# Second mixture in two halves of the tokens with 512 columns a matmul, and keys and receptances on GpSimd at the start

## The chip, the core and the metric

The kernel runs on one core of one Trainium2 chip. The metric is the device time of one execution in microseconds (us). The engines are TensorE (PE, its weight loads PEld), VectorE (DVE), ScalarE (ACT), GpSimd (POOL) and SyncE (SP), whose queue issues the DMAs.

## The reference

Three stages follow one another. `B, H, S, D = 4, 8, 768, 48`, so there are 3072 tokens of 384 features.

```python
for t in range(S):
    cur = einsum('bhd,bhe->bhde', u * kt, vt)
    y[:, :, t] = einsum('bhd,bhde->bhe', rt, state + cur)
    state = wt[..., None] * state + einsum('bhd,bhe->bhde', kt, vt)
x = y.transpose(0, 2, 1, 3).reshape(3072, 384)
x = ((x @ w1) * (x @ w2)) @ w3 @ w_out
P = exp(x @ w_gate - max)
for _ in range(8):
    P /= P.sum(1) + 1e-9; P /= P.sum(0) + 1e-9; P *= 3072 / 8
out = sum(P[:, e:e+1] * (relu(x @ ew1[e]) @ ew2[e]) for e in range(8))
```

The first mixture has 1024 hidden units; each of the 8 experts of the second has 1024 as well.

## The kernel before

**The start.** The recurrence is worked in 24 chunks of 128 tokens, and the first mixture in 8 blocks of 384 tokens. Their steps are issued in 107 slices. For the first 28 slices the table `START` (line 26) writes the order out by hand, a token a step: `L` loads an input, `ld`, `lw`, `ex`, `jn` bring a 64-bit weight to float32 (DMA, ScalarE, ScalarE, VectorE), `w34` multiplies w3 by w_out on TensorE, `scanF`, `scanG`, `small`, `ks`, `rp`, `kx`, `rx` make the decayed keys and receptances of a chunk, `sc`, `trn`, `yt1`, `up`, `yt2` are its matmuls. `ks` (line 291) and `rp` (line 296) run on VectorE, and `kx` and `rx` (from line 301) on GpSimd read what they made. The order in the program is each engine's own order: an engine that waits holds all that stands behind it.

**The second mixture.** x @ ew1 is computed as a product of two 3x3 block matrices by 15 products (`ORDER`, with the factors in `WA` and `XC`) and not 27. Each factor is split into a high and a low part in fp32r, and each product is three matmuls (high by high, high by low, low by high). The factors of x, high and low, are made once by `pre_x`, written to DRAM (`xd`) and loaded back in four groups of up to four products (`ld_x` into `xc`). The factors of w1 are made by `sp_w1` for one pair of blocks of hidden units at a time: sums on GpSimd, high parts on ScalarE, low parts on GpSimd.

A **phase** `n` works on 768 tokens (`sb`, one of 4 sets) and on two blocks of hidden units of 3 x 128 (`k`). There are 64 phases. `x2[sb]` holds a set as 9 tiles of T = 256 tokens: 3 blocks of features by 3 blocks of tokens. Each of the 15 products of a phase is two times three matmuls of 256 columns, one triple for either block of hidden units, side by side in one bank of PSUM (`z_prod`, tile `zp`; four banks). ScalarE (`cp`) and VectorE (`add`, `sub`) fold the products into the hidden layer, `h_hi` (ScalarE) and `h_lo` (VectorE) take its positive part and split it. Between the products of phase n stand the units of phase n-1 (`y_fill`): a unit is three matmuls of 384 columns, and four units close one accumulator `yp` of 128 tokens, which VectorE adds to `acc` (line 1064). There are 24 units a phase and three banks for `yp`. `later` and `spread` hang other work on the count of products done: making the weights, loading factors (`release` after each group of four products), and the gate's iteration (`sk`) in the first phases.

Of the kernel before, what the change touches and what calls it, by code (L numbers as in the profile page):

```python
# [30 lines left out]
w34.0.4 L.rn.2 kn.0 L.k.3 cp.0 w34.0.5 ex.5.0 jn.4.1 yt1.0 up.0 ex.5.1 scanF.2 w34.0.6 lw.5 w34.0.7 Sn.0 jn.5.0
yt2.0 lw.6 ld.8 L.r.3 L.rn.3 small.2 w34.1.0 L.w.3 cc.1 xraw.0 L.kn.3 sc.1 rp.2 L.v.2 jn.5.1 ex.6.0 rx.2 trn.1
w34.1.1 ws.0 ec.1 w34.1.2 jn.6.0 lw.7 w34.1.3 rk.2 cp.1 w34.1.4 ex.6.1 kn.1 w34.2.0 jn.6.1 ex.7.0 w34.1.5 w34l.0
w34.2.1 jn.7.0 lw.8 ld.10 w34.1.6 L.kn.4 ld.9 yt1.1 scanG.2 ex.8.0 w34.2.2 ex.7.1 w34.1.7 ks.2 w34.2.3 ws.1 jn.7.1
kx.2 w34.2.4 w34.2.5 w34l.1 jn.8.0 w34.3.0 ld.11 L.rn.4 w34.2.6 scanF.3 w34.2.7 ex.8.1 w34.3.1 ws.2 jn.8.1 w34.3.2
up.1 cc.2 ld.12 w34.4.0 lw.9 L.r.4 Sn.1 rk.3 w34.3.3 L.v.3 L.w.4 ex.9.0 w34.3.4 lw.10 jn.9.0 w34.3.5 ec.2 sc.2
ex.9.1 yt2.1 cc.3 scanG.3 w34.4.1 w34.4.2 lw.12 small.3 w34.4.3 rp.3 w34.3.6 xraw.1 cp.2 rx.3 w34.4.4 jn.9.1 ex.12.0
trn.2 w34l.2 lw.11 w34.4.5 jn.12.0 w34.3.7 ld.13 L.k.4 ex.10.0 w34.4.6 ks.3 ws.3 w34.4.7 jn.10.0 kx.3 L.k.5 ex.12.1
w34.5.0 L.kn.5 ws.4 L.w.5 w34.5.1 w34l.3 jn.12.1 ex.10.1 w34.5.2 rk.4 kn.2 jn.10.1 w34.5.3 ex.11.0 yt1.2 w34.5.4
jn.11.0 ex.11.1 ld.14 ec.3 L.r.5 up.2 hi.0 L.kn.6 w34.6.0 L.rn.6 Sn.2 ex.13.0 lo.0 w34.5.5 lw.13 w34.6.1 jn.11.1  # L40
w34.5.6 w34l.4 yt2.2 w34.6.2 jn.13.0 xraw.2 ld.16 w34.5.7 ld.15 scanF.4 ex.13.1 sc.3 xd.2 ws.5 w34.6.3 jn.13.1 trn.3
lw.14 w34l.5 w34.6.4 scanG.4 ex.14.0 w34.6.5 hi.1 w34.7.0 jn.14.0 L.w.6 kn.3 w34.6.6 lo.1 xh.0 w34.7.1 cp.3 w34.6.7
lw.16 small.4 w34.7.2 xl.0 yt1.3 ex.14.1 w34.7.3 ws.6 ks.4 up.3 ex.15.0 jn.14.1 kx.4 L.k.6 w34.7.4 L.v.4 w34.7.5
rp.4 hi.2 ld.17 L.v.5 w34.7.6 Sn.3 L.rn.5 lw.15 lo.2 L.r.6 w34.7.7 ex.16.0 pa.0.0 ws.7 jn.15.0 w34l.6 yt2.3 ex.15.1
jn.16.0 rx.4 asb.0.0 jn.15.1 pb.0.0 w34l.7 scanF.5 hi.3 pa.0.1 ex.16.1 lo.3 lw.17 cc.4 gs.0.0 sc.4 xraw.3 jn.16.1
# [14 lines left out]
def tile_rwkv_moe_sinkhorn_moe(  # L60
# [592 lines left out]
    def sp_w2(i):  # L653
# [3 lines left out]
        k = i % 4  # L657
        pool = pools["m" if k < 2 else "m2"]
        hi = pool.tile([P, 2, DM], F32R, tag=f"w2h{k}", name=f"w2h{k}")
        lo = pool.tile([P, 2, DM], F32R, tag=f"w2l{k}", name=f"w2l{k}")  # L660
# [34 lines left out]
    def pre_group(sb, g, tag, tmp_, eng):  # L695
        t = pools["w"].tile([P, 2, len(XP_[g][4]), T], F32R, tag=tag, name="xpre")
        sums, high, low = factors(XP_, g, XB, x2[sb], tmp_, t, eng)

        def end():
            low()  # L700
            xd[sb, g] = dram.tile(list(t.shape), F32, name=f"xd{sb}{g}")
# [535 lines left out]
```

## Time and profile before

| what | us |
|---|---|
| runs, median (lowest to highest of 3) | 1956.44 (1955.25 to 1956.48) |
| the profiled execution, its own time | 1958.0 |
| its span | 1956.2 |
| TensorE matmul busy | 1926.2 |
| VectorE, ScalarE, GpSimd busy | 1380.6, 685.7, 632.1 |
| start of the first phase of the second mixture | 446.2 |

Span is the time from the first to the last instruction; the profiled execution's own time is 1.8 us longer. TensorE's matmuls overlap, so the spacing of their starts tells what one costs, not its own duration. The granted clock is that of TensorE, as a share of 2.4 GHz.

### The profile page before, as it was taken

What the parts mean: (1) busy time and instruction counts of PE and PEld (TensorE: products, weight loads), DVE (VectorE), ACT (ScalarE), POOL (GpSimd) and SP (SyncE); (2) the same over time, 40 slices, a digit from 0 to 9 for tenths busy, and PEclk for the clock granted to TensorE, in tenths of its full rate; (3) what the DMA queues carried; (4) which work ended last, traced back from release to release, by engine and by line L of the source; (5) the groups of instructions that cost most, each with busy time, mean ns of one, the idle gap of its engine ahead of it and who ended that gap; (6) DMA issues with size and microseconds to landing.
All of it is one profiled execution on the core that took longest, in us unless ns stands there. A gap on an engine that the chain in (4) does not pass through costs nothing.

```text
span 1956.2 us, 38114 instructions
## 1 busy us (share of the span) xinstructions
PE 1926.2 (98%) x15499; PEld 1865.7 (95%) x15499; DVE 1380.6 (71%) x2419; ACT 685.7 (35%) x1320; POOL 632.1 (32%) x859
## 2 busy tenths in 40 slices
PE   6999999999999999999999999999999999999999
PEld 3689999999999999999999999999999999999999
DVE  8865777765787786666767676666676767667665
ACT  5733333344333333333323333333333333333322
POOL 4666666635331313122222222221313231312200
PEclk9999999999999999999999999999999999999999
DMA  9623444346645555555555555545455555555453
GB/s 366 219 85 96 140 132 137 103 148 240 230 171 187 186 192 192 178 198 182 194 188 187 178 199 182 190 173 204 170 195 183 190 187 190 190 178 183 171 199 120
DMA packets 90494, 353.76 MB, mean 181 GB/s; under 512 B 10384, under 2 KB 34256, under 8 KB 64592
## 3 DMA queue, kind: packets, MB, share of 16 engines
q1 hardware_dynamic: 90320, 351.34, 51.7%
q8 instruction: 122, 2.00, 0.4%
q14 instruction: 52, 0.43, 0.1%
HBM read 329.67 MB, written 20.45 MB: 179 GB/s over the span
## 4 chain that ended last, share of the span: by engine, by line
PE 94%; DMA 2%; DVE 2%; ACT 1%; issue 0%; SPq 0%; POOL 0%; DVEq 0%; ACTq 0%
PE yp L112 40%; PE zp L112 34%; PE pa L112 5%; PE po L112 5%; PE pb L112 5%; PE yt L112 1%; DMA raw<-in_moe_w_dram 1%; PE trn L112 1%; PE sc L112 1%; PE up L112 1%; DMA raw<-in_moe_w_out_dram 0%; PE w34ps L112 0%; DVE ct L892 0%; DMA nat_r<-in_rt_dram 0%; PE pl L112 0%
## 5 line engine op out<-in xcount | busy, mean ns | idle before, releaser
L112 PE MATMUL zp<-xc,w1c 128*128 128x256 f32 x5760 | 839.5, 282 | 2.0 <-DVE ct L895 1.1
L112 PEld LDWEIGHTS zp<-xc,w1c 128*128 128x128 f32 x5760 | 790.7, 188 | 16.9 <-DVE ct L895 2.9
L112 PE MATMUL yp<-w2h,hl 128*128 128x384 f32 x1536 | 516.6, 336 | 0.5 <-DVE hl L889 0.5
L112 PE MATMUL yp<-w2h,hh 128*128 128x384 f32 x1536 | 517.1, 337 | 0.0
L112 PE MATMUL yp<-w2l,hh 128*128 128x384 f32 x1536 | 514.1, 335 | 0.0
L884 ACT ACTIVATE hh<-ct 128x512 fp32r<-128x512 f32 x384 | 236.9, 632 | 601.9 <-DVE ct L895 329.0
L892 DVE TENSOR_TENSOR ct<-ct,zp 128x512 f32<-128x512 f32 x576 | 380.9, 684 | 58.1 <-PE zp L112 57.5
L614 POOL TENSOR_TENSOR w1c<-w1s,w1c 128x512 fp32r<-128x512 f32 (+1 forms) x120 | 127.2, 1060 | 787.6 <-PE zp L112 475.7
L899 ACT ACTIVATE ct<-zp 128x512 f32<-128x512 f32 x256 | 153.4, 599 | 397.9 <-PE zp L112 393.9
L112 PEld LDWEIGHTS yp<-w2h,hh 128*128 128x128 f32 x1536 | 290.7, 189 | 0.2 <-issue 0.2
L112 PEld LDWEIGHTS yp<-w2h,hl 128*128 128x128 f32 x1536 | 288.1, 188 | 0.9 <-DVE hl L889 0.8
L112 PEld LDWEIGHTS yp<-w2l,hh 128*128 128x128 f32 x1536 | 288.5, 188 | 0.0
L889 DVE SCALAR_TENSOR_TENSOR hl<-ct,hh 128x512 fp32r<-128x512 f32 x384 | 273.8, 727 | 0.0
L1064 DVE SCALAR_TENSOR_TENSOR acc<-yp,Pm,acc 128x384 f32<-128x384 f32 x336 | 205.3, 611 | 69.9 <-PE yp L112 69.8
L895 DVE TENSOR_TENSOR ct<-ct,zp 128x512 f32<-128x512 f32 x128 | 88.1, 688 | 170.2 <-PE zp L112 170.1
L895 DVE TENSOR_TENSOR ct<-zp,ct 128x512 f32<-128x512 f32 x128 | 88.4, 691 | 135.9 <-PE zp L112 131.0
L614 POOL TENSOR_TENSOR w1c<-w1raw,w1c 128x128 fp32r<-128x128 f32 (+1 forms) x90 | 55.0, 611 | 221.4 <-ACT w1c L610 221.4
L606 POOL TENSOR_TENSOR w1s<-w1raw 128x128 f32<-128x128 f32 x240 | 120.1, 521 | 0.2
L481 POOL TENSOR_TENSOR gl<-gs,gh 128x384 fp32r<-128x384 f32 x64 | 73.3, 1147 | 111.1 <-ACT gh L477 111.1
L112 PE MATMUL pa<-xhl,w1h 128*128 128x384 f32 x384 | 102.2, 347 | 0.0
L112 PE MATMUL pb<-xhl,w2h 128*128 128x384 f32 x384 | 98.9, 338 | 2.3 <-DVE cv L228 2.3
L472 DVE TENSOR_TENSOR gs<-pb,asb 128x384 f32<-128x384 f32 x64 | 35.4, 554 | 72.3 <-PE pb L112 52.7
(128 smaller groups left out, 1900.6 us busy)
## 6 DMA issues: line engine op xcount, KB each, us to landing
xc<-xd SPq DMA_DIRECT2D x192, 1024.0 KB, 4.9
xc<-xd SPq DMA_DIRECT2D x64, 768.0 KB, 4.3
xd<-x2s SPq DMA_DIRECT2D x53, 256.0 KB, 2.9
w1raw<-in_e_w_dram SPq DMA_DIRECT2D x32, 384.0 KB, 3.1
w2raw<-in_e_w_dram SPq DMA_DIRECT2D x32, 384.0 KB, 3.1
raw<-in_moe_w_dram SPq DMA_DIRECT2D x8, 1024.0 KB, 8.5
nat_w<-in_w_dram SPq DMA_DIRECT2D x24, 264.5 KB, 3.5
nat_k<-in_kt_dram SPq DMA_DIRECT2D x24, 256.0 KB, 4.1
```

The costliest lines, as they stand in the source:

```text
L112: nc.tensor.matmul(o, lhsT, rhs, start=start, stop=stop, **kw)
L472: nc.vector.tensor_tensor(t, m_t.pop(("pb", blk, f)), m_t.pop(("asb", blk, f)), op=ALU.mult)
L481: nc.gpsimd.tensor_tensor(gl[:, f, :], m_t.pop(("gs", blk, f)), gh[:, f, :].bitcast(F32), op=ALU.subtract)
L606: eng.tensor_tensor(tmp_[:, many.index(r), :], at_(a), at_(b), op=ALU.add if sg == 1 else ALU.subtract)
L614: eng.tensor_tensor(lo[:, d0:d1, :], sv, hi[:, d0:d1, :].bitcast(F32), op=ALU.subtract)
L884: nc.scalar.activation(hh, src, AF.Relu)
L889: nc.vector.scalar_tensor_tensor(hl, src, 0.0, hh.bitcast(F32), op0=ALU.max, op1=ALU.subtract)
L892: nc.vector.tensor_tensor(o, a, b_, op=ALU.add)
L895: nc.vector.tensor_tensor(o, a, b_, op=ALU.subtract)
L899: nc.scalar.activation(t, src, AF.Copy)
L1064: nc.vector.scalar_tensor_tensor(dst, yp, so["Pm"][:, tt, e:e + 1], dst, op0=ALU.mult, op1=ALU.add)
```

## The change

The second mixture now works on two sets of 1536 tokens (`SS = 2 * S`) with T = 512, and a phase has one block of hidden units `p`. `SEQ` lists the 64 phases: two blocks on one set, the same two on the other, then the next two blocks starting from the set at hand, so the factors of x are loaded at every second phase and shared by two. A product is three matmuls of 512 columns. A unit of `y_fill` is still three matmuls of 384 columns, and two of them close an accumulator, of which there are 12 a phase. The even ones go to VectorE as before. The odd ones (but for the last phase's) go through ScalarE, scaled by the gate, into one of two pieces of a work tile `xw`, and GpSimd adds that to `acc`. The weights' factors have two sets, not three, and w1's and w2's raw tiles one, not two; one set's factors of x are made on VectorE during the first mixture, the other's on VectorE and, from slice 90 into the third phase, on GpSimd.

At the start `ks` and `rp` of the first five chunks go to GpSimd, the two copies of the unit block go to ScalarE, and `START` is another list.

```diff
+KS_POOL = (0, 1, 2, 3, 4)
+RP_POOL = (0, 1, 2, 3, 4)
 START = """
-L.w.0 L.w.1 L.k.0 ld.0 L.r.0 ld.1 L.kn.1 L.k.1 L.r.1 scanG.0 scanF.0 ks.0 scanG.1 lw.0 ld.2 ld.3 L.kn.0 ex.0.0
...
+L.w.0 L.k.0 ld.0 L.w.1 L.r.0 ld.1 scanG.0 scanF.0 ks.0 ex.0.0 ld.2 small.0 ld.3 lw.0 L.kn.0 scanG.1 L.rn.0 rp.0
...
-    T = 256
-    NR = S // T
-    NS = B
+    T = 512
+    SS = 2 * S
+    NR = SS // T
+    NS = NT // SS
...
-        nc.gpsimd.tensor_copy(eye[64 * c:64 * c + 64, :], ident[64 * c:64 * c + 64, 64 * c:64 * c + 64])
+        nc.scalar.activation(eye[64 * c:64 * c + 64, :], ident[64 * c:64 * c + 64, 64 * c:64 * c + 64], AF.Copy)
...
-        nc.vector.tensor_tensor(diag(t), nat["k", n % 2].rearrange("p (a b s) -> p b a s", b=2, s=32), gv, op=ALU.mult)
+        (nc.gpsimd if n in KS_POOL else nc.vector).tensor_tensor(diag(t), nat["k", n % 2].rearrange("p (a b s) -> p b a s", b=2, s=32), gv, op=ALU.mult)
...
+    SEQ = [(2 * k + j, sb) for k in range(NB2) for sb in ((0, 1), (1, 0))[k % 2] for j in range(2)]
+    N = len(SEQ)
...
+    B_DVE = (2, 13, 7, 9)
...
+    B_AT = {6: (90.75, 91.75, 92.75, 2), 15: (93.75, 94.75, 95.75, 3), 8: (99.25, 99.5, 100.75, 2),
+            5: (101.25, 101.5, 102.75, 3), 2: (100.75, 102.25, 103.25, 0), 13: (102.75, 104.25, 105.25, 1),
+            7: (104.75, 106.25, 107, 0), 9: (114, 115, 116, 0), 10: (114, 114, 115, 1), 11: (123, 124, 125, 1),
+            1: (119, 123, 124, 0), 12: (127, 130, 131, 1), 4: (126, 129, 130, 0), 3: (133, 136, 137, 1),
+            14: (132, 135, 136, 0)}
...
-        return pools["z"].tile([P, 2, T], F32, tag="z", bufs=4, name="zp")
+        return pools["z"].tile([P, T], F32, tag="z", bufs=4, name="zp")
...
-        xt = xc[n, g]
-        for j in range(2):
-            wt = w1c[(n // NS) * 2 + j, g]
-            for c, (a_, b_) in enumerate(((0, 0), (0, 1), (1, 0))):
-                mm(bank[:, j, :], wt[:, a_, wi, :], xt[:, b_, xi, :], start and j == 0 and c == 0,
-                   stop and c == 2, skip=True)
+        wt, xt = w1c[SEQ[n][0], g], xc[n, g]
+        for c, (a_, b_) in enumerate(((0, 0), (0, 1), (1, 0))):
+            mm(bank, wt[:, a_, wi, :], xt[:, b_, xi, :], start and c == 0, stop and c == 2, skip=True)
...
+                two = t % 2 and n < N - 1
...
+                elif two:
+                    yt_n[0] += 1
+                    c0 = T * (yt_n[0] % 2)
+                    tm = xw_part(c0, c0 + DM)
+                    if e == 0:
+                        nc.scalar.activation(tm, yp, AF.Copy)
+                    else:
+                        nc.scalar.activation(tm, yp, AF.Copy, scale=so["Pm"][:, tt, e:e + 1])
+                    nc.gpsimd.tensor_tensor(dst, dst, tm, op=ALU.add)
...
     def release(n, g):
...
-        ld_x(n + 1, g)
-        if sb == NS - 1:
-            spread(1, 3 if g == 2 else 2, sp_w1(2 * k + 3, g, nc.gpsimd))
+        p, sb = SEQ[n]
+        if n + 1 < N:
+            if SEQ[n + 1][1] == sb:
+                xc[n + 1, g] = xc[n, g]
+            elif n == 1 and g > 1:
+                later(29 + g - at["slot"], lambda: ld_x(n + 1, g))
+            else:
+                ld_x(n + 1, g)
+        if n % 4 > 1 and p + 2 < NW:
+            spread(12 if p % 2 else 1, 3, lazy(lambda: sp_w1(p + 2, g, nc.gpsimd)))
```

TensorE's order inside a late phase, with the z matmuls (`zp`) of two products and the units of the phase before it between them. Before:

```order
L112 MATMUL zp<-xc_19674,w1c_19084 128x256 x3
L112 MATMUL zp<-xc_19674,w1c_19677 128x256 x3
L112 MATMUL yp<-w2h_18174,hh 128x384
L112 MATMUL yp<-w2l_18175,hh 128x384
L112 MATMUL yp<-w2h_18174,hl 128x384
L112 MATMUL zp<-xc_19674,w1c_19084 128x256 x3
```

With the change:

```order
L115 MATMUL zp<-xc_16211,w1c_16440 128x512 x3
L115 MATMUL yp<-w2h,hh 128x384
L115 MATMUL yp<-w2l,hh 128x384
L115 MATMUL yp<-w2h,hl 128x384
L115 MATMUL zp<-xc_16211,w1c_16440 128x512 x3
```

Two triples of 256 columns, with the weights of two blocks, became one triple of 512 columns with one block's weights; the units between them are the same.

ScalarE's order in a late phase, where `hh` is the hidden layer's high half, `ct` a product taken out of PSUM, `w1c` weights and `xw` the work tile. Before:

```order
L899 ACTIVATE ct<-zp 128x512 x4
L610 ACTIVATE w1c_21538<-w1s 128x512
L884 ACTIVATE hh<-ct 128x512 x2
```

With the change:

```order
L912 ACTIVATE ct<-zp 128x512
L620 ACTIVATE w1c_18174<-xw 128x512
L1083 ACTIVATE xw<-yp,Pm 128x384
L897 ACTIVATE hh<-ct 128x512 x2
L1083 ACTIVATE xw<-yp,Pm 128x384
L897 ACTIVATE hh<-ct 128x512
L620 ACTIVATE w1c_18224<-w1raw 128x128
L620 ACTIVATE w1c_18224<-w1s 128x384
```

The copies of the odd accumulators (`xw<-yp,Pm`) now stand between the products, weights and hidden halves.

GpSimd's order at the very start, where `Kt` and `Rt` are a chunk's keys and receptances. Before:

```order
L136 AFFINE_SELECT mask<-mask 64x64
L304 TENSOR_TENSOR Kt<-Kt,Mt 128x8x32
L304 TENSOR_TENSOR Kt<-Kt,Ft 128x8x32
L310 TENSOR_TENSOR Rt<-Rt,Mt 128x8x32
L310 TENSOR_TENSOR Rt<-Rt,Ft 128x8x32
```

With the change:

```order
L139 AFFINE_SELECT mask<-mask 64x64 x2
L297 TENSOR_TENSOR Kt<-nat_k_101,Gt 128x2x8x32
L301 TENSOR_TENSOR Rt<-nat_r_99,Ft 128x2x8x32
L307 TENSOR_TENSOR Kt<-Kt,Mt 128x8x32
L307 TENSOR_TENSOR Kt<-Kt,Ft 128x8x32
L313 TENSOR_TENSOR Rt<-Rt,Mt 128x8x32
L313 TENSOR_TENSOR Rt<-Rt,Ft 128x8x32
```

The first chunk's `ks` (`Kt<-nat_k`) and `rp` (`Rt<-nat_r`) now stand on GpSimd ahead of the four halves that read them; on VectorE they are gone.

## Rows read from the trace of the kernel before

**Rows 1.** The page: engines, busy us (share) and instructions; shares of the ending chain.

```profile
PE 1926.2 (98%) x15499; PEld 1865.7 (95%) x15499; DVE 1380.6 (71%) x2419; ACT 685.7 (35%) x1320; POOL 632.1 (32%) x859
...
PE 94%; DMA 2%; DVE 2%; ACT 1%; issue 0%; SPq 0%; POOL 0%; DVEq 0%; ACTq 0%
```

**Rows 2.** Stretches: us, each engine's busy us (instructions), granted clock, DMA share, GB/s.

```profile
core 0: us, PE busy (x) PEld busy (x) DVE busy (x) ACT busy (x) POOL busy (x), PEclk, DMA share, GB/s
...
80.00:90.00 10.00, 7.68 (x91) 7.14 (x91) 9.13 (x19) 7.64 (x16) 9.21 (x9) 0.83 0.57 179
...
110.00:120.00 10.00, 8.81 (x222) 7.67 (x220) 6.49 (x20) 4.07 (x9) 9.92 (x12) 1.00 0.30 86
120.00:446.20 326.20, 326.20 (x3873) 308.31 (x3873) 227.58 (x485) 122.12 (x286) 183.78 (x174) 1.00 0.38 121
446.20:600.00 153.80, 151.53 (x1053) 147.80 (x1052) 114.99 (x219) 57.19 (x116) 62.29 (x92) 1.00 0.63 220
600.00:1900.00 1300.00, 1299.84 (x9078) 1287.93 (x9076) 903.59 (x1460) 420.91 (x775) 311.01 (x509) 1.00 0.53 187
1000.00:1200.00 200.00, 200.00 (x1397) 198.35 (x1396) 140.40 (x224) 66.22 (x124) 52.52 (x87) 1.00 0.54 188
```

**Rows 3.** TensorE in order of time, a late phase: start us, us, what.

```profile
1501.57 0.34 PE L112 MATMUL yp<-w2h,hh 128*128 128x384 f32 x1
...
1502.62 0.87 PE L112 MATMUL zp<-xc,w1c 128*128 128x256 f32 x6
1503.32 0.34 PE L112 MATMUL yp<-w2h,hh 128*128 128x384 f32 x1
```

**Rows 4.** TensorE in order of time, the end, 39 steps from first to last.

```profile
1945.57 0.33 PE L112 MATMUL yp<-w2h,hl 128*128 128x384 f32 x1
...
1952.33 0.34 PE L112 MATMUL yp<-w2h,hl 128*128 128x384 f32 x1
```

**Rows 5.** Groups, whole span: what, count | busy us, mean ns | idle before, releasers.

```profile
L1064 DVE SCALAR_TENSOR_TENSOR acc<-yp,Pm,acc 128x384 f32<-128x384 f32 x336 | 205.3, 611 | 69.9 <-PE yp L112 69.8
L606 POOL TENSOR_TENSOR w1s<-w1raw 128x128 f32<-128x128 f32 x240 | 120.1, 521 | 0.2
L481 POOL TENSOR_TENSOR gl<-gs,gh 128x384 fp32r<-128x384 f32 x64 | 73.3, 1147 | 111.1 <-ACT gh L477 111.1
L614 POOL TENSOR_TENSOR w1c<-w1s,w1c 128x512 fp32r<-128x512 f32 x30 | 39.4, 1314 | 787.6 <-PE zp L112 475.7 <-ACT w1c L610 311.9
L468 ACT ACTIVATE asb<-pa 128x384 f32<-128x384 f32 x64 | 31.4, 491 | 42.6 <-PE pa L112 39.5 <-DVE gs L472 3.1
L319 POOL TENSOR_TENSOR ec<-eye,cc 128x512 f32<-128x512 f32 x24 | 29.7, 1236 | 7.6 <-PE po L112 7.6
L294 DVE TENSOR_TENSOR Kt<-nat_k,Gt 128x512 f32<-128x512 f32 x24 | 18.1, 756 | 0.1
L298 DVE TENSOR_TENSOR Rt<-nat_r,Ft 128x512 f32<-128x512 f32 x24 | 17.1, 712 | 0.6 <-DMA nat_r<-in_rt_dram 0.6
```

**Rows 6.** TensorE in order of time, the first 84 us, where it stood still.

```profile
10.83 1.13 PE L112 MATMUL sc<-Rt,Kt 64*64 64x64 f32 x32 [10.83 <-POOL Rt L310]
...
19.41 6.97 PE L112 MATMUL w34ps<-wo,w3c 128*128 128x384 f32 x12 [6.40 <-DVE w3c L228]
...
30.97 0.91 PE L112 MATMUL w34ps<-wo,w3c 128*128 128x384 f32 x2 [1.39 <-DVE w3c L228]
...
83.10 0.96 PE L112 MATMUL pb<-xhl,w2h 128*128 128x384 f32 x2 [2.32 <-DVE cv L228]
```

**Rows 7.** ScalarE in order of time, its first instruction.

```profile
8.44 1.28 ACT L209 ACT_TABLE_LOAD   x1 [8.44 <-DMA raw<-in_moe_w_out_dram]
```

**Rows 8.** The page: DMA issues, count, KB each, median us to landing.

```profile
xc<-xd SPq DMA_DIRECT2D x192, 1024.0 KB, 4.9
xc<-xd SPq DMA_DIRECT2D x64, 768.0 KB, 4.3
```

More of the change, by code (lines that the diff above doesn't have):

```diff
@@ L31 @@
[L31 to L45, printed above, removed]
@@ L656, in sp_w2 @@
         t = w2raw.pop(i)
[L657 to L660, printed above, removed]
+        hi, lo = (pools["m2" if i % 2 else "m"].tile([P, 2, DM], F32R, tag=f"w2{x}{i % 2}", name="w2" + x) for x in "hl")
         nc.scalar.activation(hi, t, AF.Copy)
@@ L693, in pre_x @@
         return sums, high, low
[L695 to L701, printed above, removed]
-            nc.sync.dma_start(xd[sb, g], t.bitcast(F32))
-        return sums, high, end
+    SEQ = [(2 * k + j, sb) for k in range(NB2) for sb in ((0, 1), (1, 0))[k % 2] for j in range(2)]
+    N = len(SEQ)
     def ld_x(n, g):
-        if n >= NB2 * NS:
-            return
         t = x_tile(n, g)
-        nc.sync.dma_start(t.bitcast(F32), xd[n % NS, g])
+        nc.sync.dma_start(t.bitcast(F32), xd[SEQ[n][1], g])
     slices = {}
@@ new lines, in tile_rwkv_moe_sinkhorn_moe, with make @@
+    for r_, (s_, (a_, b_)) in A_AT.items():
+        if len(XC[r_]) == 3:
+            at_ = (s_ + 0.5, s_ + 0.75, s_ + 1.75)
+        else:
+            at_ = (s_ + 0.75, s_ + 2.75, s_ + {3: 3.75, 2: 4.5}[s_ % 4])
+        place(at_[0], lazy(lambda r_=r_, a_=a_, b_=b_: pre_x(0, r_, x2w[0][:, a_:b_ + 1:b_ - a_, :], nc.vector)),
+              at_[1], at_[2])
+    B_AT = {6: (90.75, 91.75, 92.75, 2), 15: (93.75, 94.75, 95.75, 3), 8: (99.25, 99.5, 100.75, 2),
[4 rows of a table added]
+    b_task = {}
+    for r_, (*at_, w_) in B_AT.items():
+        def make(r_=r_, w_=w_):
+            return pre_x(1, r_, work(w_), nc.vector if r_ in B_DVE else nc.gpsimd)
+        b_task[r_] = lazy(make)
+        for f_, s_ in zip(b_task[r_], at_):
+            if s_ < NSL:
+                event(s_, f_)
@@ L826, in tile_rwkv_moe_sinkhorn_moe @@
             ld_w1(0)
-            ld_w1(1)
+            for g in range(2):
+                ld_x(0, g)
             st_pa.close()
@@ L910, in spread @@
     def spread(d, lag, task):
-        if task:
-            sums, high, end = task
-            later(d, sums)
-            later(d + lag, high, end)
+        sums, high, end = task
+        later(d, sums)
+        later(d + lag, high)
+        later(d + lag + 1, end)
     PO = 9
@@ L1035, in phase, with unit @@
             h_lo(n, 0, 1)
+    yt_n = [0]
     def y_fill(n):
-        k, sb = divmod(n, NS)
-        e, dp = divmod(k, NDP)
+        p, sb = SEQ[n]
+        e = p // NPR
         yt = {}
-        def unit(b_, h_, i, j):
-            first = i == 1 and j == 0
-            last = i == 0 and j == 1
-            if first:
+        def unit(b_, h_, i):
+            if i == 1:
                 yt[b_, h_] = pools["y"].tile([P, DM], F32, tag="y", bufs=3, name="yp")
@@ L1064, in unit @@
                     nc.vector.scalar_tensor_tensor(dst, yp, so["Pm"][:, tt, e:e + 1], dst, op0=ALU.mult, op1=ALU.add)
-                if k == NB2 - 1:
+                if p == NPR - 1:
+                    e0_done.add((sb, t))
+                if p == NW - 1:
                     nc.sync.dma_start(out[tt * P:(tt + 1) * P, :], dst)
         for b_ in (0, 2, 1):
-            for h_ in range(2):
-                for i in (1, 0):
-                    for j in range(2):
-                        yq.append(lambda b_=b_, h_=h_, i=i, j=j: unit(b_, h_, i, j))
+            us = [(h_, i) for h_ in range(T // P) for i in (1, 0)]
+            if b_ == 1:
+                us[5], us[6] = us[6], us[5]
+            for h_, i in us:
+                yq.append(lambda b_=b_, h_=h_, i=i: unit(b_, h_, i))
+    e0_done = set()
     def release(n, g):
```

204 lines of the change are left out of this document (112 added, 92 removed), and 3 rows, old and new, of the table XAT.

## The prediction

> **What bounds the kernel now.** I read the engines and the chain first [rows 1]: TensorE is busy 98% of the span and holds 94% of the chain that ended last. So the time is TensorE's work plus the few places where it stood still, and the change has to be read there. The stretches [rows 2] show where those places are: before 120 us, and a little from 446 to 600 us, where the gate's iteration runs beside the first phases. From 600 to 1900 us TensorE has 1299.84 of 1300 us at a granted clock of 1.00, which is the 2.4 GHz level. There VectorE is busy 70%, ScalarE 32%, GpSimd 24%. In that stretch only a shorter TensorE program saves time; every other edit can only cost.
>
> A phase is 90 z matmuls and 72 y matmuls, 162 in all, so 1397 in 200 us [rows 2] make a phase of 200 / 1397 x 162 = 23.19 us. Six y matmuls of 384 columns start within 1.05 us, 0.175 us each [rows 3]; 72 of them are 12.60 us. That leaves 10.59 us for the z matmuls, 0.706 us for the six of one product; the rows show 0.70 us [rows 3].
>
> **The z matmuls.** Each product's six matmuls of 256 columns become three of 512; products, phases (64) and y matmuls (72 a phase) stay. No row has 512 columns, so I bound one. At 2.4 GHz 256 columns are 106.7 ns and 384 are 160.0 ns. The z matmuls stand at 0.706 / 6 = 117.7 ns, 11 ns above their columns. The y matmuls stand at 175 ns between z matmuls, 15 ns above, but at 173.3 ns where y alone is left, 39 of them from 1945.57 to 1952.33 us [rows 4], 13 ns above. If that excess belongs to the matmul whatever its width, three of 512 (213.3 ns each) cost 0.673 us with 11 ns and 0.685 us with 15. With 13 ns they cost 0.679 us, 0.027 us less than now. Over 64 x 15 = 960 products that is **-26 us** (-32 to -20). The other end is a straight line through 117.7 and 175 ns, 57.3 ns per 128 columns: 232.3 ns, 0.697 us a product, only -9 us. I take 13 ns, the excess of the undisturbed 384 columns, the nearest width; the line stays as a rival.
> The Trainium skill (TensorE: Matmul & The Clock Gate, "Wait — 56ns, not 53.3ns?") speaks against this: it gives a warm matmul its columns at 2.4 GHz plus a fixed 2.5 ns or so. By it the halved count would save 3 x 2.5 ns a product, an estimate of 7 us in all. The trace disagrees on the size: its excess is 11 to 15 ns.
>
> **Emptying y.** An accumulator now gets one block of hidden units and not two, so it closes after 6 matmuls: 12 evictions a phase, not 6. The even ones stay on VectorE: 6 a phase at 0.61 us, as now [rows 5]. The odd six go through ScalarE into a work tile and are added by GpSimd. Nearest rows: ScalarE's 128x384 out of PSUM, 0.49 us, and GpSimd's 128x384 with two inputs, 1.15 us [rows 5]. ScalarE goes from 0.32 x 23.2 = 7.5 to 10.4 us a phase, GpSimd from 5.5 to 12.4 us, of about 22.8. Both are under 55%, so I cost this at **nothing**. Its cover is the three y banks: a bank is wanted again two groups (about 3.8 us) after its group closed. If ScalarE came later than that, TensorE would stand; ScalarE's products and hidden halves queue behind the same copy.
>
> **Weights and factors.** Splitting w1 costs GpSimd the same work, one block every two phases. In a quarter with four sums it is 4 x 0.52 + 1.31 us [rows 5]: 3.4 us at a stretch, in front of the y adds. One set in place of three leaves over a phase between last use and next need. The x factors are now loaded at every second change of block, 16 times and not 64, in pieces of 2048 KB and 1536 KB. From 768 to 1024 KB a load gains 0.6 us [rows 8], so 2048 KB would take 4.9 + 4 x 0.6 = 7.3 us. A group is released 11 or 12 products (17 us) before the next phase wants it. **Nothing**, except once: the last factors of the second half are finished by GpSimd at the 30th product, written out, and loaded for the 38th. One low half (1.3 us), a 512 KB write (I take 3.7 us, between nothing and the 768 KB row) and a 2048 KB load make 12.3 us against 8 x 1.5 = 12 us. **+2 us** (0 to 6). Making the factors is mostly VectorE work of the same columns in half as many instructions, under TensorE's full stretch [rows 2]. The rescaling of the accumulators is bunched, up to 9 in a phase; at VectorE's 0.61 us each [rows 5] its 16.1 us become 21.6 and still fit in 22.8.
>
> **The first 28 slices.** Ten products of keys and receptances leave VectorE (0.76 and 0.71 us each [rows 5]) for GpSimd, whose 128x512 with two inputs takes 1.24 us [rows 5]. TensorE's first large stop is 6.40 us until VectorE's first piece of w3 is there [rows 6]; four of the ten (2.9 us) stood ahead of it and no longer do. Later it stops 1.39 us and 2.32 us for VectorE again [rows 6], and after the second the granted clock is 0.83 for 10 us [rows 2], 1.7 us more, since TensorE fell to 1.2 GHz after standing still. All of it gone is -8.3 us. Against that the ten are 0.5 us longer each on GpSimd, which scores, keys and gates wait for: +5 us if all lie on the path. GpSimd is at 99% from 110 to 120 us [rows 2]. The list is new throughout, so I take a bit over the middle of -8 and +5 towards the gain, as VectorE is the releaser in the rows: **-5 us**. The two copies of the unit block move to ScalarE, which has 8.44 us of nothing before its table load [rows 7]: nothing.
>
> **Sum**, against the profiled execution's 1958.0 us (span 1956.2): 1958.0 - 26 - 5 + 2 = 1929.0. The median of the runs is 1.6 us lower, so **1927 us**; the ends -32 - 8 + 0 and -20 + 5 + 6 give 1916 to 1947.
>
> **Rivals.**
> *The excess grows with the columns.* For it: 15 ns at 384 against 11 at 256 [rows 2, 3]. Against it: 13 ns where 384 columns run alone [rows 4], so 2 of the 15 come from the alternation. Then 1958.0 - 9 - 5 + 2 - 1.6 = 1944 us. A fixed cost of 2.5 ns, the page's rule above, would end at about the same place.
> *The y adds hold ScalarE (slower than before).* The place: the copy of an odd group needs a work tile that GpSimd gave back, and there are two. GpSimd's longest lump is 3.4 us plus an add, 4.5 us; the next copy but one comes 7.6 us later. It decides once GpSimd runs over 3.1 us late: then ScalarE stands, the bank stays full, TensorE stands. Some 30 phases hold w1 splits, four lumps each: 120 lumps. At 0.25 us each the gain is gone; at 0.4 us it is 1927 + 48 = 1975 us. For it: two engines in file order and a hand-off that TensorE did not have. Against it: both have half their time free.
> *GpSimd becomes the bound of the first 120 us.* The list then costs +4 and not -5: 1936 us. For it: 99% from 110 to 120 us [rows 2]. Against it: the ten lie ahead of that stretch.
> *The large x loads come late.* If each of 15 changes cost 2 us, 1957 us, no change. Against it: 7.3 us against 17.
> That the change doesn't do what it says can be left out: the built order has three 128x512 per product.
>
> **Chances.** Forecast 0.68; excess per column 0.12; GpSimd bound at the start 0.08; late loads 0.05; y adds 0.07. A measurement can tell about 0.2%, 4 us. Forecast, columns and start are faster (0.88), and some late loads with them: faster 0.90, same 0.04, slower 0.06. The range leaves out most of the y adds and late loads and the tips of the others: 1914 to 1944 us.
>
> **What would show it.** Right: 2880 z matmuls of 128x512, 226 ns apart; about 22.8 us a phase, so some 1028 matmuls in 200 us of the steady stretch; TensorE still at 100% there; the first w34 matmul near 16.5 us and no clock under 1.00 around 80 us; GpSimd near 55%, ScalarE near 45%. The column rival shows as 232 ns with TensorE still full. The y rival shows as TensorE idle, released by ScalarE, in front of y matmuls, and ScalarE waiting for GpSimd's adds. The start rival shows as TensorE waiting for GpSimd before 120 us. Late loads show as z matmuls that wait for a DMA every fourth phase. I am wrong if TensorE stands over 5 us in the steady stretch.

## The result, and the profile after

The changed kernel takes 1982.94 us (median of 4 runs, 1980.68 to 1984.14), the kernel before 1956.46 us beside it: a ratio of 1.0137, 95% interval 1.0125 to 1.0149. It is 1.4% **slower**; the forecast was 1927 us, its range 1914 to 1944. The profiled execution took 1982.3 us, with a span of 1980.6.

The page of the changed kernel: engines and chain first, then groups (what, count | busy us, mean ns | idle before, releasers) and DMA issues (count, KB, us to landing).

```profile
PE 1928.0 (97%) x12619; PEld 1735.5 (88%) x12619; DVE 1448.4 (73%) x2361; ACT 879.7 (44%) x1662; POOL 1068.3 (54%) x1231
...
PE 84%; DVE 8%; DMA 3%; ACT 3%; issue 1%; POOL 1%; SPq 0%; DVEq 0%; ACTq 0%; POOLq 0%
...
L1084 POOL TENSOR_TENSOR acc<-acc,xw 128x384 f32<-128x384 f32 x366 | 416.7, 1139 | 678.6 <-ACT xw L1083 513.1
L115 PE MATMUL zp<-xc,w1c 128*128 128x512 f32 x2112 | 606.0, 395 | 17.1 <-ACT ct L912 12.5
...
L905 DVE TENSOR_TENSOR ct<-ct,zp 128x512 f32<-128x512 f32 x576 | 380.2, 682 | 74.0 <-PE zp L115 71.8
...
L902 DVE SCALAR_TENSOR_TENSOR hl<-ct,hh 128x512 fp32r<-128x512 f32 x384 | 344.4, 910 | 6.2 <-ACT hh L897 6.2
L1083 ACT ACTIVATE xw<-yp,Pm 128x384 f32<-128x384 f32 x330 | 189.9, 575 | 318.6 <-PE yp L115 312.0
...
xc<-xd SPq DMA_DIRECT2D x51, 2048.0 KB, 8.1
...
xd<-x2s SPq DMA_DIRECT2D x15, 512.0 KB, 3.8
```

There are 2880 fewer matmuls, and TensorE is as long busy as before [rows 1]: each z costs more than was forecast. TensorE holds 84% of the chain, not 94%. So there is new standing too. Its stretches (columns as in [rows 2]) and its longest waits:

```profile
446.00:600.00 154.00, 138.32 (x692) 121.16 (x690) 108.78 (x204) 59.98 (x118) 67.05 (x77) 0.96 0.41 148
1000.00:1200.00 200.00, 198.95 (x1006) 179.99 (x1005) 150.62 (x222) 94.61 (x176) 112.10 (x140) 1.00 0.26 95
```
```profile
engine line waited for: us in total, times, longest us
PE zp L115 <- ACT ct L912: 21.4, 20, 10.4
```

From 446 to 600 us TensorE stands 15.7 us where it stood 2.3 [rows 2], at a mean clock of 0.96. In the steady stretch it stands 1.05 us in 200, and it does 1006 matmuls where 1028 were forecast. Most of what TensorE waits for in the phases is `ct` (line 912): ScalarE's copy of a z bank, which is due before the next product may add to that bank.

The first z matmul of each phase (every 45th) gives the phases' lengths. I count phases from one.

| phase | before, us | after, us |
|---|---|---|
| start of the first | 446.2 | 441.0 |
| 1 | 28.36 | 31.72 |
| 3 | 24.06 | 37.31 |
| 9, 10, 11 | 23.16, 23.12, 23.10 | 24.80, 27.69, 24.01 |
| 12 to 63, most | 23.1 to 23.5, mean 23.21 | 23.07 to 23.14 |
| of these 14, 18, ... 62 | the same | 23.82 to 23.85 |

The span grew by 24.4 us: -5.2 at the start, +25.2 in phases 1 to 11, +3.8 in phases 12 to 63, +0.6 from the start of the last phase to the end.

Three places show who holds whom. The **third phase**, in order of time (start us, us, what, and in brackets the idle time before it and its releaser), with the DMA issues of that stretch:

```profile
489.02 1.29 POOL L701 TENSOR_TENSOR xw<-x2s 128x512 f32<-128x512 f32 x1 [5.00 <-DMA xd<-xw]
...
499.79 1.26 POOL L701 TENSOR_TENSOR xw<-x2s 128x512 f32<-128x512 f32 x1 [6.98 <-DMA xd<-xw]
...
502.43 0.63 ACT L705 ACTIVATE xw<-xw 128x512 fp32r<-128x512 f32 x1 [4.81 <-POOL xw L701]
...
505.46 0.63 ACT L705 ACTIVATE xw<-xw 128x512 fp32r<-128x512 f32 x1 [1.88 <-POOL xw L701]
...
506.36 0.59 ACT L912 ACTIVATE ct<-zp 128x512 f32<-128x512 f32 x1
...
507.00 1.22 PE L115 MATMUL zp<-xc,w1c 128*128 128x512 f32 x2 [10.36 <-ACT ct L912]
```
```profile
xc<-xd SPq DMA_DIRECT2D x3, 2048.0 KB, 9.0
xd<-xw SPq DMA_DIRECT2D x6, 512.0 KB, 6.4
```

Read it from the bottom: TensorE waits for ScalarE's copy; ScalarE has been held in front of it by the high half of a late x factor; that half waits for GpSimd's sum; GpSimd waits to write into a work tile whose last content is still on its way to DRAM. Those 512 KB writes stand beside 2048 KB loads and take 6.4 us here, 3.8 elsewhere.

Such a stop costs more than its own length. Two stretches of the same trace, in the third and in the tenth phase (columns as in [rows 2]), and two y matmuls inside the first:

```profile
498.60:512.20 13.60, 5.20 (x14) 4.62 (x15) 2.74 (x7) 3.81 (x8) 7.92 (x6) 0.50 0.27 101
682.90:686.30 3.40, 3.40 (x11) 3.02 (x11) 3.05 (x6) 0.80 (x2) 2.50 (x3) 0.50 0.12 32
```
```profile
508.45 0.52 PE L115 MATMUL yp<-w2h,hh 128*128 128x384 f32 x1
508.77 0.52 PE L115 MATMUL yp<-w2l,hh 128*128 128x384 f32 x1
```

The granted clock is 0.50 there, the 1.2 GHz level, and the y matmuls are 0.32 us apart and not 0.175. Of the 5.20 and 3.40 us that TensorE worked at that level, half is lost: an estimate of 2.6 us in the third phase and 1.7 in the tenth.

**Every fourth phase**, here the one that starts at 1521.2 us:

```profile
1520.23 1.83 ACT L897 ACTIVATE hh<-ct 128x512 fp32r<-128x512 f32 x3 [1.69 <-DVE ct L905]
1521.97 0.40 ACT L620 ACTIVATE w1c<-w1raw 128x256 fp32r<-128x256 f32 x1
1522.27 0.29 ACT L620 ACTIVATE w1c<-w1s 128x128 fp32r<-128x128 f32 x1
1522.47 0.56 ACT L1083 ACTIVATE xw<-yp,Pm 128x384 f32<-128x384 f32 x1
1522.94 0.58 ACT L912 ACTIVATE ct<-zp 128x512 f32<-128x512 f32 x1
...
1523.57 0.97 PE L115 MATMUL zp<-xc,w1x 128*128 128x512 f32 x3 [0.46 <-ACT ct L912]
```

Two high parts of the next w1 stand in the queue just where a phase's first copy is due. The **tenth phase**:

```profile
676.76 1.45 POOL L1084 TENSOR_TENSOR acc<-acc,xw 128x384 f32<-128x384 f32 x1
...
677.27 1.16 DVE L1168 TENSOR_SCALAR acc<-acc,Pm 128x384 f32<-128x384 f32 x1
...
679.06 1.23 ACT L897 ACTIVATE hh<-ct 128x512 fp32r<-128x512 f32 x2 [4.02 <-DVE ct L905]
679.55 0.41 DVE L1168 TENSOR_SCALAR acc<-acc,Pm 128x384 f32<-128x384 f32 x1
...
681.12 0.40 ACT L620 ACTIVATE w1c<-w1raw 128x256 fp32r<-128x256 f32 x1
681.43 0.29 ACT L620 ACTIVATE w1c<-w1s 128x128 fp32r<-128x128 f32 x1
...
682.64 1.44 PE L115 MATMUL zp<-xc,w1x 128*128 128x512 f32 x3 [2.73 <-ACT ct L912]
```

There the rescalings (L1168) make VectorE late, ScalarE waits for VectorE, and TensorE for ScalarE; the two high parts of w1 stand in front of the copy here too. The same rescaling takes 1.16 us beside an add on GpSimd and 0.41 without one.

### The profile page after: what moved, and what is told of

Its sections match the earlier page's. It is cut to its first block, busy times and chain, and to the rows that moved or that the text cites. A ratio compares the mean times of both kernels' runs of the same rounds, so it can differ in the third digit from the quotient of the medians.

```text
span 1980.6 us, 32609 instructions
## 1 busy us (share of the span) xinstructions
PE 1928.0 (97%) x12619; PEld 1735.5 (88%) x12619; DVE 1448.4 (73%) x2361; ACT 879.7 (44%) x1662; POOL 1068.3 (54%) x1231
## 4 chain that ended last, share of the span: by engine, by line
PE 84%; DVE 8%; DMA 3%; ACT 3%; issue 1%; POOL 1%; SPq 0%; DVEq 0%; ACTq 0%; POOLq 0%
PE yp L115 35%; PE zp L115 30%; PE po L115 5%; PE pa L115 5%; PE pb L115 4%; DVE ct L905 2%; DVE hl L902 2%; PE w34ps L115 1%; PE yt L115 1%; DMA xd<-xw 1%; ACT hh L897 1%; DMA xw<-in_e_w_dram 1%; PE trn L115 1%; PE sc L115 1%; DMA nat_kn<-in_kn_dram 1%
## 5 line engine op out<-in xcount | busy, mean ns | idle before, releaser
L1084 POOL TENSOR_TENSOR acc<-acc,xw 128x384 f32<-128x384 f32 x366 | 416.7, 1139 | 678.6 <-ACT xw L1083 513.1
L115 PE MATMUL zp<-xc,w1c 128*128 128x512 f32 x2112 | 606.0, 395 | 17.1 <-ACT ct L912 12.5
L905 DVE TENSOR_TENSOR ct<-ct,zp 128x512 f32<-128x512 f32 x576 | 380.2, 682 | 74.0 <-PE zp L115 71.8
L115 PEld LDWEIGHTS zp<-xc,w1c 128*128 128x128 f32 x2112 | 384.1, 188 | 56.1 <-ACT ct L912 14.2
L902 DVE SCALAR_TENSOR_TENSOR hl<-ct,hh 128x512 fp32r<-128x512 f32 x384 | 344.4, 910 | 6.2 <-ACT hh L897 6.2
L1083 ACT ACTIVATE xw<-yp,Pm 128x384 f32<-128x384 f32 x330 | 189.9, 575 | 318.6 <-PE yp L115 312.0
L115 PE MATMUL zp<-xc,w1x 128*128 128x512 f32 x768 | 224.3, 400 | 9.6 <-ACT ct L912 8.8
L115 PEld LDWEIGHTS zp<-xc,w1x 128*128 128x128 f32 x768 | 136.0, 188 | 32.6 <-ACT ct L912 14.0
```

Of the source, the lines that this page charges most:

```text
L115: nc.tensor.matmul(o, lhsT, rhs, start=start, stop=stop, **kw)
L902: nc.vector.scalar_tensor_tensor(hl, src, 0.0, hh.bitcast(F32), op0=ALU.max, op1=ALU.subtract)
L905: nc.vector.tensor_tensor(o, a, b_, op=ALU.add)
L1083: nc.scalar.activation(tm, yp, AF.Copy, scale=so["Pm"][:, tt, e:e + 1])
L1084: nc.gpsimd.tensor_tensor(dst, dst, tm, op=ALU.add)
```

## The experiments

The runs were taken in rounds, each with the kernel before beside it, whose median lay between 1955.0 and 1957.0 us; a difference of medians from two rounds can be off by that much, and the ratios are to before of the same round.

**Which part.** The start alone on the kernel before, and the mixture alone:

> The kernel before with the new start alone (keys and receptances of five chunks on GpSimd, unit block on ScalarE, new list). If the start itself gains: first phase some 4 us earlier than 446.2 us, the time about 1952 us. If the earlier first phase of the changed kernel came from the lighter VectorE work in the first mixture: 1956 us, no change.

> The changed kernel with the old start. If start and second mixture add up: 1987 us, 4 us over the changed kernel. If the start does not matter: 1983 us. Three phases hold most of the loss: the third phase some 37 us long, the eleventh some 28 us.

The start alone took 1952.63 us (11 runs), 0.9984 of before (0.9976 to 0.9993); its first phase starts at 441.1 us. The mixture alone took 1985.12 us, 1.0154 (1.0139 to 1.017), with the third phase 37.37, the tenth 27.66 (the text above calls it the eleventh), every fourth 23.85 us. So the start gains some 3 us by the medians, and all the loss is the mixture's.

**The width.** The changed kernel with each z matmul cut into two of 256 columns, and a stream of matmuls by itself:

```diff
-            mm(bank, wt[:, a_, wi, :], xt[:, b_, xi, :], start and c == 0, stop and c == 2, skip=True)
+            mm(bank[:, js], wt[:, a_, wi, :], xt[:, b_, xi, js], start and j == 0 and c == 0,
+               stop and c == 2, skip=True)
```

> The changed kernel with each z matmul of 512 columns cut into two of 256. If the width is what I forecast (a fixed excess of 13 ns): 6 x 118 against 3 x 227, 960 products, +27 us, 2010 us. If 512 columns cost 231.5 ns as the spacing in the changed kernel reads: 0.708 against 0.695 us a product, +13 us, 1996 us. If width does not matter at all: 1983 us.

> Nothing of the reference is computed; zeros are written. TensorE alone streams fp32r matmuls of 128, 256, 320, 384, 448, 496 and 512 columns, each with new weights, then 512 and 384 columns in alternation, then the same beside GpSimd adds and beside VectorE adds. If the excess at 512 columns is the matmul's own: 384 columns stand at 173 ns and 512 at 231 to 236 ns with every other engine idle, and neither moves when GpSimd or VectorE run. If the excess comes from the company in SBUF: 512 columns stand at 226 ns alone and at 231 or more beside GpSimd.

Cut in two, the kernel takes 1987.53 us, 1.0161 (1.0147 to 1.0175). So 512 columns in place of 256 are worth 4.6 us by the medians, whose intervals overlap, and not 26. The spacing agrees: in phases 17 to 48, stops left out, a z matmul of 256 columns stands at 118.5 ns and a y at 174.0, one of 512 columns at 233.3 and its y at 175.4. That is 45 x 3.7 - 72 x 1.4 = 66 ns a phase, some 4 us. The stream tells why. Alone, a width settles at 120.0 ns for 256 columns, 173.3 for 384 and 226.7 for 512 (starts of the records): 13.3 ns over the columns at each of the three. (It is 13.3 at 320 too, but 20.0 at 448, 16.6 at 496 and 58.4 at 128.) But 3 of 512 in turn with 6 of 384 took 1760 ns, where these figures make 3 x 226.7 + 6 x 173.3 = 1720; beside adds on GpSimd or on VectorE it was the same. A second stream varied the length of the runs:

> Nothing of the reference is computed, zeros are written: matmuls of 512 and 384 columns in turn, new weights each, in runs of 1 and 2, 3 and 6, 6 and 12, 12 and 24, 24 and 48 matmuls; then 3 of 448 with 6 of 384, 3 of 512 with 6 of 256, 6 of 256 with 6 of 384. Theory (every change of width costs over the next six to ten matmuls): 3 of 512 with 6 of 384 take 1755 to 1765 ns in the shortest runs and fall towards 1720 ns with the length, below 1732 at 24 and 48. Rival (the mixture costs whatever its order): 1750 ns or more at every length.

The stretches of that stream: 1 and 2 in turn (96 matmuls), then 3 and 6, 6 and 12, 12 and 24, 24 and 48 (144 in each; the counts also take in one or two at the edges).

```profile
32.28:51.05 18.77, 18.77 (x97) 17.45 (x97) 0.00 (x0) 0.00 (x0) 0.00 (x0) 1.00 0.00 0
51.05:79.21 28.16, 28.16 (x145) 26.00 (x145) 0.00 (x0) 0.00 (x0) 0.00 (x0) 1.00 0.00 1
79.21:107.00 27.79, 27.79 (x146) 25.68 (x145) 0.00 (x0) 0.00 (x0) 0.00 (x0) 1.00 0.00 1
107.00:134.78 27.78, 27.78 (x145) 25.74 (x145) 0.00 (x0) 0.00 (x0) 0.00 (x0) 1.00 0.00 1
134.78:162.44 27.66, 27.66 (x146) 25.70 (x145) 0.00 (x0) 0.00 (x0) 0.00 (x0) 1.00 0.00 1
```

Nine matmuls take 1760 ns in runs of 1 and 2 and of 3 and 6, 1737 in runs of 6 and 12 and of 12 and 24, 1729 in runs of 24 and 48. In the long runs, after a change to 512 the starts are 229, 233, 236, 224, 231, 236, 228, 233, 230 ns apart and then 227; after one to 384, 171, 175, 178, 185, 176, 181 and then 173. So the excess belongs to the **change of width**, and it is not one price per change: going there and back costs 13 ns in runs of 1 and 2, 40 in runs of 3 and 6, 33 in runs of 6 and 12, and 66 where the runs are long enough to settle. It is not so for every pair: 3 of 448 with 6 of 384 took 1660 ns, which is what they take alone (206.7 and 173.3), and 6 of 256 with 6 of 384 no more than alone, 1753 or 1754 ns for 1760. In the kernel before, then, the change of width was free, and in the new one it is not.

**The y adds.** Every y eviction back on VectorE (`two = False`):

> The changed kernel, but every y eviction on VectorE: no copy of y by ScalarE, no add by GpSimd. Theory (GpSimd's adds slow VectorE's operations that read two operands from SBUF and the copies load ScalarE, hence the stall of 0.77 us in every fourth phase): hl from 0.91 us back to 0.73 to 0.80, the pattern of every fourth phase gone, VectorE near 85%, total 1972 to 1977 us if VectorE's added 3.7 us a phase fit. Rival (VectorE becomes the bound with twelve adds of 0.61 us): phases above 23.5 us throughout, total above 1990 us.

It took 1978.69 us, 1.0115 (1.01 to 1.013): 4 us less by the medians, though the intervals overlap, and `hl` fell from 910 to 782 ns. But every fourth phase stayed at 23.7 to 23.8 us, the third at 37.81, and ScalarE's `ct` is still what TensorE waits for:

```profile
PE zp L115 <- ACT ct L912: 19.0, 20, 10.3
```

So the adds are not what holds ScalarE, and twelve evictions a phase do not make VectorE the bound. Both theories fell; the rows of every fourth phase point at the w1 high parts.

**The stalls, one by one.** The late factors first: the last four of the second set (products 3, 12, 14, 4) are made straight in `xc`, with sums in pieces of their own, and only the others of those two groups are loaded. Their places move too: the sums of 3 and 14 come earlier, the high halves of 12, 4 and 14 later.

```diff
+        def high():
+            nc.scalar.activation(xc[2, g][:, 0, xi, :], sv, AF.Copy)
+        def low():
+            nc.gpsimd.tensor_tensor(xc[2, g][:, 1, xi, :], sv, xc[2, g][:, 0, xi, :].bitcast(F32), op=ALU.subtract)
...
-            1: (119, 123, 124, 0), 12: (127, 130, 131, 1), 4: (126, 129, 130, 0), 3: (133, 136, 137, 1),
-            14: (132, 135, 136, 0)}
+            1: (119, 123, 124, 0), 12: (127, 134, 135, 2), 4: (126, 137, 138, 0), 3: (128, 135, 136, 3),
+            14: (130, 138, 139, 4)}
...
-                later(29 + g - at["slot"], lambda: ld_x(n + 1, g))
+                t = x_tile(2, g)
+                for r in ORDER[4 * g:4 * g + 4]:
+                    if r not in DIRECT:
+                        nc.sync.dma_start(t[:, :, i_, :].bitcast(F32), xd[1, g][:, :, i_, :])
```

> The changed kernel, but the last four late x factors of the second half are made straight in the tile that TensorE reads, not written to DRAM and loaded back as a group. Theory (GpSimd waited for DMA writes that queued beside 2048 KB loads, ScalarE waited for GpSimd, TensorE for ScalarE): third phase 24 to 26 us instead of 37.3, first-phase lengths and the later ones unchanged, total 1970 to 1973 us. Rival (the third phase is long because GpSimd has too much work there, or because loads are short of bandwidth in any order): third phase stays above 32 us, total above 1978 us.

1970.15 us, 1.0071 (1.0056 to 1.0086): **12.8 us less**, the third phase 25.52 us. That the late factors held that phase is shown; the edit takes the write and the load back out of that path, and with them the shared pieces and the old places, and no run parts these. The clock stays at 1.00, and with it the tenth phase falls to 26.13 us, although TensorE's stop there is as long as in the changed kernel (2.72 us, and 2.73): the 1.6 us that it lost less agree with the estimate for the clock. What is left in the third phase is one wait:

```profile
497.30 0.97 PE L115 MATMUL zp<-xc,w1c 128*128 128x512 f32 x3 [1.78 <-ACT ct L937]
```

Then the rescalings (the second half's moved, every other one of the first half's given to ScalarE), alone and together with the late factors and an earlier load of w2:

```diff
-                    later((1, 3, 5, 7, 9, 11, 32, 34, 36, 38, 40, 42)[m], lambda m=m: rescale(1, TB[m]))
+                    later((1, 3, 5, 7, 9, 11, 46, 48, 50, 52, 54, 56)[m], lambda m=m: rescale(1, TB[m]))
...
+        if sb == 0 and t % 2:
+            nc.scalar.activation(dst, dst, AF.Copy, scale=so["Pm"][:, tt, 0:1])
```
```diff
+    ld_w2(0)
     ld_x(0, 2)
     ld_x(0, 3)
-    ld_w2(0)
```

> The changed kernel, but six of the second half's twelve rescalings go from the tenth phase to the eleventh, and every other one of the first half's twelve goes to ScalarE. Theory (rescalings bunched on a VectorE that is slower beside GpSimd hold TensorE): the tenth phase 23.2 to 24.5 us instead of 27.7, ninth not over 24.5, total 1977 to 1980 us. Rival (the stall comes from GpSimd's y adds or the weights' split, whatever VectorE does): tenth phase stays above 26.5 us, total 1982 to 1984 us.

> Both edits of the two runs before and the second layer's first weights loaded ahead of the last two x groups. Theory (the losses add up, each in its own phase): first phase 28.5 to 30 us instead of 31.7, third 24 to 26, tenth 23.2 to 24.5, total 1962 to 1968 us. Rival (one stall takes another's place): phases saved in one place come back within the next two, total above 1972 us.

The rescalings moved give 1978.58 us, 1.0111 (1.0095 to 1.0128), 4.4 us less by the medians, whose intervals overlap; the tenth phase is 24.74 us, a little above what was expected, and its clock stays at 1.00, so by that some 1.6 of the 2.95 us that it got shorter are the clock's. The three edits give 1965.94 us, 1.0048 (1.0033 to 1.0063), and the first phase 29.57 us. The gains add up if the tenth phase's 1.6 us are not counted twice: 12.8 and 4.4, less 1.6, and 1.5 for the first phase (31.08 with the late factors only) make 17.1, and 17.0 were measured with all three.

Then the one place of the w1 split (its fourth quarter, in every second block, three products earlier), on top of the three and on the changed kernel alone:

```diff
-            spread(12 if p % 2 else 1, 3, lazy(lambda: sp_w1(p + 2, g, nc.gpsimd)))
+            spread((12 if g < 3 else 9) if p % 2 else 1, 3, lazy(lambda: sp_w1(p + 2, g, nc.gpsimd)))
```

> The kernel with the three edits of the run before, and the fourth quarter of every second block's w1 split three products earlier, so that ScalarE's two high parts no longer stand ahead of its first copy of a phase. Theory (those 0.40 + 0.29 us keep the first z bank of every fourth phase, 0.77 us lost each time): every fourth phase 23.0 to 23.3 us instead of 23.8, total 1954 to 1958 us. Rival (the hidden halves that wait for VectorE are what holds ScalarE there): every fourth phase stays above 23.6 us, total 1964 to 1967 us.

> The changed kernel with nothing but that one place moved (fourth quarter of every second block's w1 split three products earlier). Theory: every fourth phase 23.0 to 23.3 us, total 1971 to 1976 us. Rival: 23.8 us still, total 1981 to 1985 us.

Alone it gives 1972.28 us, 1.0079 (1.0064 to 1.0095): **10.7 us less** for one number, with every fourth phase 23.14 us and the tenth 25.14. The same place in its trace, in the phase that starts at 1514.9 us:

```profile
1513.55 1.83 ACT L897 ACTIVATE hh<-ct 128x512 fp32r<-128x512 f32 x3 [1.31 <-DVE ct L905]
1515.28 0.56 ACT L1083 ACTIVATE xw<-yp,Pm 128x384 f32<-128x384 f32 x1
1515.76 0.60 ACT L912 ACTIVATE ct<-zp 128x512 f32<-128x512 f32 x1
```

The copy starts 2.21 us after the hidden halves and not 2.71, as two high parts less stand between them. The halves themselves start 0.36 us earlier in the phase, since VectorE is earlier there too (GpSimd's part of the split moved with the rest; whether that is the reason, no run tells). So 0.5 of the 0.86 us are the queue's. In the tenth phase the gains do not add up: this edit alone brings it to 25.14 us, the rescalings alone to 24.74, all four to 24.56.

All four edits give 1954.66 us (11 runs), 0.9993 (0.9984 to 1.0002), no difference from before. Their groups and their steady stretch:

```profile
L927 DVE SCALAR_TENSOR_TENSOR hl<-ct,hh 128x512 fp32r<-128x512 f32 x384 | 356.3, 941 | 0.0
```
```profile
1000.00:1200.00 200.00, 200.00 (x1015) 181.74 (x1014) 152.81 (x224) 93.28 (x172) 106.47 (x130) 1.00 0.26 95
```

TensorE is full again, though `hl` on VectorE is as slow as ever. What is left of the missing gain is the width.

**The width, in the kernel.** The four edits stay, and only the table that gives out the y units is changed, so that z products stand together. The first row is that of the four, the second makes nine runs of z in a phase in place of fifteen, the third seven:

```diff
-    YN = dict(zip(ORDER, (2, 2, 1, 2, 2, 1, 1, 1, 2, 1, 2, 2, 2, 1, 99)))
+    YN = dict(zip(ORDER, (2, 2, 0, 3, 2, 0, 3, 0, 3, 0, 3, 0, 3, 0, 99)))
+    YN = dict(zip(ORDER, (2, 2, 0, 3, 2, 0, 0, 4, 0, 0, 5, 0, 0, 0, 99)))
```

> The kernel with the four edits, and the same y matmuls given out so that six times in a phase two products of z stand together (nine runs of z in a phase instead of fifteen). Theory (a change from 384 to 512 columns and back costs 33 to 40 ns, as in the stream alone): six fewer in a phase are 0.2 to 0.24 us, phases of 22.85 to 22.95 us instead of 23.07 to 23.14, total 1941 to 1947 us. Rival (the excess has nothing to do with the change of width, or VectorE's and ScalarE's work on two products at once holds TensorE): phases not under 23.05 us, total 1953 us or more.

> The same with seven runs of z in a phase, up to four products together. Theory of the width alone: eight fewer changes, 22.75 to 22.87 us a phase, total 1937 to 1943 us. Rival (four z banks and VectorE at 73% can't take three or four products in 3 us): TensorE stands in every phase for VectorE, phases above 23.2 us, total above 1955 us. I expect the rival here, since VectorE needs 0.7 us for each z bank and again 0.9 for each hidden low half.

I had these the wrong way round. Nine runs took 1965.67 us, 1.0054 (1.0041 to 1.0066): every other phase is 22.86 us, as the width says, and the ones between 23.4 to 23.9. ScalarE's first copy of a phase is late again, behind hidden halves that wait for VectorE:

```profile
1134.18 1.83 ACT L922 ACTIVATE hh<-ct 128x512 fp32r<-128x512 f32 x3 [1.30 <-DVE ct L930]
1135.92 0.56 ACT L1108 ACTIVATE xw<-yp,Pm 128x384 f32<-128x384 f32 x1
1136.38 0.58 ACT L937 ACTIVATE ct<-zp 128x512 f32<-128x512 f32 x1
```
```profile
1137.02 0.95 PE L115 MATMUL zp<-xc,w1x 128*128 128x512 f32 x3 [0.57 <-ACT ct L937]
```

The table leaves three y units behind the last two products, which stand together. The four edits leave two, with one more between those products, and do not stand; so the number of units alone does not explain it, and no run parts it from the grouping. Seven runs leave six units behind the last four products, and took **1942.74 us** (5 runs), 0.9936 (0.9922 to 0.9949): faster than both kernels. Its steady stretch and one of its runs of z:

```profile
1000.00:1200.00 200.00, 200.00 (x1020) 182.04 (x1020) 147.44 (x222) 94.24 (x176) 109.96 (x138) 1.00 0.26 95
```
```profile
1501.09 2.25 PE L115 MATMUL zp<-xc,w1c 128*128 128x512 f32 x9
1503.18 0.34 PE L115 MATMUL yp<-w2h,hh 128*128 128x384 f32 x1
```

Over phases 17 to 48 a z matmul costs 230.7 ns from start to start, and 232.9 with the four edits; a y matmul 174.6 and 175.5. Per phase that is 45 x 2.2 + 72 x 0.9 = 164 ns. Phases 12 to 63 together are 8.3 us shorter and the first eleven 3.1, of the 11.9 us between the two medians. VectorE could take four products in a row with six units behind them: the price that I set on it did not fall due there.

## Why the prediction was wrong

- **The z matmuls** (-26 us) failed at "if that excess belongs to the matmul whatever its width". Alone it does, 13.3 ns at 256, 384 and 512 columns. In the kernel, in turn with 384, 512 columns cost 232.9 ns with the four edits. I read 13 ns from 384 columns alone [rows 4] and carried it to 512 columns in company, and took the y spacing of 175 ns as fixed, though the y matmuls bear part of the cost. The steady phase fell by some 0.1 us, not 0.41. The rival with 232 ns was right in size and wrong in cause. The Trainium skill (TensorE: Matmul & The Clock Gate, "Wait — 56ns, not 53.3ns?") gives a fixed 2.5 ns or so; the stream shows 13.3 ns at 256, 320, 384 and 512 columns, more at 128, 448 and 496, and beyond it a cost that hangs on what stood before.
- **The late factors** (+2 us) measured about 13: the edit that makes them in place, places included, took 12.8 away. I summed a low half, a write and a load on the way to the loads' deadline, and no load missed it. What was missed is the queue: GpSimd behind the write, ScalarE behind GpSimd, and behind ScalarE's high half the copies that TensorE needs; and then the clock, an estimate of 2.6 us in this phase and 1.6 us measured in the tenth, for which this term had nothing. The write's 3.7 us was right for a write alone (3.8) and not beside 2048 KB loads.
- **Weights and factors, "Nothing"** measured 10.7 us (the one moved place). The lengths were right and there was time enough in the phase; two high parts of 0.40 and 0.29 us stood in ScalarE's order in front of the first copy of the phase, which makes some 0.5 of the 0.86 us by which that copy was late; the rest came by way of VectorE. What counts is the place, not the share: ScalarE is 44% busy.
- **The rescalings** ("still fit in 22.8") measured 4.4 us (the rescalings moved). I added busy times over a phase at 0.61 us each; they came in lumps, and beside GpSimd one took up to 1.18 us. Some 1.6 us of the gain are the clock's, by the tenth phase of the run with the late factors.
- **Emptying y, "nothing"**: nearly right. Giving it all back to VectorE gains 4 us by the medians, at the edge of what the runs can tell. The chain of its rival (ScalarE waits for a tile that GpSimd holds) came true, but with the x factors' tile and a DMA at its end, and not with the y adds.
- **The start** (-5 us): right within its bounds, 3 us by the medians on the kernel before. The first large stop fell from 6.40 us [rows 6] to 2.58 and the first phase starts 5.2 us earlier. The first `w34` matmul came at 17.77 us, not 16.5, and the very first matmul 2.2 us later than before (13.01 us, released by GpSimd): keys and receptances on GpSimd do lie on the path there.

Of the 53 us between the sum (1929) and the profiled 1982.3, the z matmuls' term makes some 20, the late factors 11, the w1 place 11, the rescalings 4 and the first weights of w2 some 2. The other 5 or so were not run down. These shares overlap where two edits meet in the tenth phase.

## What to carry to other kernels

Where several engines each run in file order, a share of busy time under 55% covers nothing by itself: look at what stands in the queue directly in front of the copy that TensorE waits for, and follow that instruction's own wait to its end, DMAs included. A matmul's price is to be measured in the sequence in which it will run, with the widths that stand before and behind it. And when a new tiling seems to give nothing, undo its stalls one at a time by the phase: here four small edits gave back 28 us, and the order of the same matmuls 12 more. Look at the clock in the stalled stretch as well: part of what an edit seems to gain is the clock that it keeps.
